# A gated recurrence feeding a squared-ReLU MLP: y with tokens as rows and then transposed, against y formed in channels

## The chip, the cores and the metric

The kernel runs on one core of a Trainium2 chip. TensorE multiplies matrices: it loads up to 128x128 stationary weights (PEld in the profile) and streams a moving operand past them into PSUM. VectorE (DVE), ScalarE (ACT) and GpSimd (POOL) work on tiles, and DMA queues, most of them issued by SyncE (SP), move data. The metric is device microseconds from start to end of one execution. Before the change the median of three runs is 202.72 us (202.46 to 202.79).

## The reference

Four batches, eight heads, 768 steps, head size 48; the outputs of the recurrence are the 3072 tokens of an MLP with 384 channels and 2048 hidden units.

```python
def _attn_ref(q, k, v, alpha):
    state = np.zeros((B, H, D, D))
    for t in range(S):
        state = alpha[:, :, t, :, None] * state + np.einsum('bhd,bhe->bhde', k[:, :, t], v[:, :, t])
        y[:, :, t] = np.einsum('bhd,bhde->bhe', q[:, :, t], state)

def _moe_ref(x, w_in, w_out, s, b):
    h = x @ w_in
    r = np.maximum(h, 0.0)
    g = s * (r * r) + b
    return g @ w_out
```

## The kernel before, in words

**Blocks.** The 768 steps of a batch are cut into six chunks of 128 tokens, so there are 24 blocks, `n = 0..23`, with chunk number `c = n % 6`. A block's recurrence is done with matrix products. The weights w_in and w_out are loaded once, cast to bf16 and kept.

**One block.** `ln` (ScalarE) takes the logarithm of alpha; `cum` sums it over the tokens with a triangular matmul and ScalarE forms exp(-sum) and exp(sum), L233 and L234; `qk` (VectorE, L250 and L251) scales k and q with them; `tr` transposes q and k to have channels as partitions (eight TensorE transposes, L256, one VectorE copy, L261); `amat` forms the products A of q and k, 128x128 for each head, with two heads side by side in the rows of the array (L271), and VectorE masks them into `am_sb` (L279). `vcast` (GpSimd, L211 and L215) casts v to bf16 into two zero-padded tiles.

**y and the state.** `inter` (L287, not for c = 0) and `yp` (L306) make y directly with channels as partitions in the bank `y_ps`. For `inter` the state of the chunk before, spread with zeros over six 128x128 slices of `sd_sb`, is the weight and the transposed q is moving: six matmuls of 128 columns. For `yp` the padded v is the weight (64 columns, so two matmuls run beside each other in two halves of the array's columns) and A is moving: twelve matmuls of 128 columns. For c < 5, eight small matmuls (L331) form each head's product of k and v in `p_ps`; `state` adds it to the decayed state (VectorE, L350 or L352) and GpSimd scales it (L358, L364, L371). ScalarE copies y to `xd_sb` (L339). Because of the padding, the order of y's channels differs from that of x, and the rows of w_in are loaded in the same order: `load_w_in` cuts w_in into two halves of columns and each half into four DMAs by rows.

**The MLP.** For a unit u = 0..3 of a block, `mp` computes four hidden tiles of 128 into a bank of `h_ps` (two in turn; twelve matmuls, L393), `rl` is the ReLU on ScalarE (L407), `sq` the square on VectorE (L414), and `mm2` (called as `o`) adds four of the sixteen products with w_out into `o_ps` (L428). After the last unit VectorE adds the bias row (L441), or, for the first five blocks, ScalarE keeps the sum (L437) until the bias is known.

**Order.** Each engine runs its instructions in the order in which they are written. That order is fixed by hand: a list for the first four blocks, with positions 0.1 apart, and formulas after that, with eight positions for a block (p = 8n). From block 8 on, between y(n) at p and y(n+1) at p + 8 lie amat(n+1) at p + 0.1, o(n-1,0) at p + 0.5, cum(n+2) at p + 1.2, m(n,0) at p + 1.5, then o and m in turn, and tr(n+2) at p + 5.2. `busy(i)` puts i matmuls without a use (L197) where TensorE would stand still early on. Loads for eight blocks are in flight on SP's queue; w_in follows blocks 0 and 1, with its second half between the four loads of block 2.

Of the kernel before, what the change touches and what calls it, by code (L numbers as in the profile page):

```python
# [14 lines left out]
def kernel(  # L20
# [165 lines left out]
    def bias_row():  # L186
        for part, c0, c1 in ((p_ps[:, 192:512], 0, 320), (y_ps[:, 384:448], 320, 384)):
            nc.tensor.matmul(out=part, lhsT=ones_f, rhs=cs_sb[:, 0, c0:c1], start=True, stop=True)
            nc.scalar.activation(out=bias_w[:, c0:c1], in_=part, func=AF.Copy, scale=b_col)
# [19 lines left out]
    def vcast(n):  # L209
        vs = v_sb[n % NLD]  # L210
        nc.gpsimd.tensor_copy(  # L211
            out=vp_sb[n % 3].rearrange("s h (a b) -> s h a b", b=4)[:, :, :, 0:3],
            in_=vs[:, 0:6].rearrange("s h (a b) -> s h a b", b=3),
        )
        nc.gpsimd.tensor_copy(  # L215
            out=vz_sb[n % 3].rearrange("s e t (a b) -> s e t a b", b=4)[:, :, :, :, 3],
            in_=vs[:, 6:8].rearrange("s e (a t) -> s e t a", t=3),
        )
# [62 lines left out]
    def inter(n):  # L281
        if n % NCH == 0:
            return
        sd = sd_sb[(n - 1) % 2]
        for i in range(6):
            p, kk = (i, i) if i < 3 else (3, i - 3)
            nc.tensor.matmul(  # L287
                out=y_ps[:, 128 * kk : 128 * kk + 128],
                lhsT=sd[0:112, i, :],
                rhs=qkT_sb[n % 2][0:112, 0, p, :],  # L290
                start=(i == 0),
                stop=False,
                skip_group_check=True,
            )

# [3 lines left out]

    def yp(n):  # L300
        c = n % NCH
        first = [c == 0, c == 0]

        def y(h, kk, lhsT, last):
            e = h % 2
            nc.tensor.matmul(  # L306
                out=y_ps[64 * e : 64 * e + 64, 128 * kk : 128 * kk + 128],
                lhsT=lhsT,
                rhs=am_sb[e][n % 2][:, h // 2, :],
                start=first[e],  # L310
                stop=last,
                skip_group_check=True,
            )
            first[e] = False

        for kk in range(3):
            for e in range(2):
                y(2 * kk + e, kk, vp_sb[n % 3][:, 2 * kk + e, :], False)
        for kk in range(3):
            for e in range(2):  # L320
                y(6 + e, kk, vz_sb[n % 3][:, e, kk, :], True)
        if c < NCH - 1:
            kb = kb_sb[n % 3]
            for p in range(NP):
                for e in range(2):
                    h = 2 * p + e
                    if h < 6:
                        rhs = vp_sb[n % 3][:, h].rearrange("s (a b) -> s a b", b=4)[:, :, 0:3]
                    else:
                        rhs = vz_sb[n % 3][:, e].rearrange("s t (a b) -> s t a b", b=4)[:, :, :, 3]  # L330
                    nc.tensor.matmul(  # L331
                        out=pst[64 * e : 64 * e + 48, p, :],
                        lhsT=kb[:, h, 0:48],
                        rhs=rhs,
                        start=True,
                        stop=True,
                    )
# [1 line left out]
        nc.scalar.activation(  # L339
            out=xd_sb[g][:, :, i * C : (i + 1) * C],  # L340
            in_=y_ps[:, 0:384].rearrange("a (t s) -> a t s", t=KT),
            func=AF.Copy,
        )
        if c < NCH - 1:
            state(n)

    def state(n):
        c = n % NCH
        if c == 0:
            nc.vector.tensor_copy(out=t1_sb[0:112], in_=pst[0:112])  # L350
        else:
            nc.vector.tensor_tensor(out=t1_sb[0:112], in0=pst[0:112], in1=sc_sb[0:112], op=ALU.add)  # L352
        bl = blast[n % 3]
        sd = sd_sb[n % 2]
        for e in range(2):
# [2 lines left out]
            nc.gpsimd.tensor_tensor(  # L358
                out=cols[:, 0:3, :, 0:3],
                in0=t1_sb[r, 0:3].rearrange("k p (a b) -> k p a b", b=3),  # L360
                in1=bl[r, 0:3].unsqueeze(3).to_broadcast([48, 3, 16, 3]),
                op=ALU.mult,
            )
            nc.gpsimd.tensor_tensor(  # L364
                out=cols[:, 3:6, :, 3],
                in0=t1_sb[r, 3].rearrange("k (t a) -> k t a", t=3),
                in1=bl[r, 3:4].to_broadcast([48, 3, 16]),
                op=ALU.mult,
            )
# [218 lines left out]
```

## Time and profile before

| what | value |
|---|---|
| median of three runs | 202.72 us |
| the profiled execution: its time | 202.63 us |
| its span, first to last instruction | 200.9 us |
| granted TensorE clock, mean | 0.996 |
| VectorE busy | 149.4 us, 74% |
| ScalarE busy | 106.5 us, 53% |
| GpSimd busy | 77.6 us, 39% |
| HBM read, written | 25.19 MB, 4.74 MB |

A matmul's time in the profile runs until its result is out, and the next one starts long before that. So the time that a matmul occupies the array is read from the distance between starts, not from its own length. Idle time of an engine costs nothing unless somebody waits for what it does next.

### The profile page before, as it was taken

What the parts mean: (1) busy time and instruction counts of PE and PEld (TensorE: products, weight loads), DVE (VectorE), ACT (ScalarE), POOL (GpSimd) and SP (SyncE); (2) the same over time, 40 slices, a digit from 0 to 9 for tenths busy, and PEclk for the clock granted to TensorE, in tenths of its full rate; (3) what the DMA queues carried; (4) which work ended last, traced back from release to release, by engine and by line L of the source; (5) the groups of instructions that cost most, each with busy time, mean ns of one, the idle gap of its engine ahead of it and who ended that gap; (6) DMA issues with size and microseconds to landing.
All of it is one profiled execution on the core that took longest, in us unless ns stands there. A gap on an engine that the chain in (4) does not pass through costs nothing.

```text
span 200.9 us, 6383 instructions
## 1 busy us (share of the span) xinstructions
PE 187.6 (93%) x2574; PEld 146.4 (73%) x2577; DVE 149.4 (74%) x289; ACT 106.5 (53%) x211; POOL 77.6 (39%) x171
## 2 busy tenths in 40 slices
PE   1979899999988999999999999999999999999992
PEld 1546588765775788888788878888878887888771
DVE  6456687788699779999886877887777787796341
ACT  3225486663557464655555565465565556544440
POOL 8364332530620078437530633641701463362000
PEclk9999999999999999999999999999999999999998
DMA  7999999999999546939695965983998591111102
GB/s 127 194 301 300 241 231 380 226 196 191 173 190 170 80 73 90 204 78 195 120 233 125 227 115 109 185 132 70 219 173 136 85 186 40 43 39 42 41 5 76
DMA packets 112608, 30.35 MB, mean 151 GB/s; under 512 B 106675, under 2 KB 111810, under 8 KB 112578
## 3 DMA queue, kind: packets, MB, share of 16 engines
q1 hardware_dynamic: 112574, 29.94, 74.6%
q8 instruction: 20, 0.33, 0.8%
q14 instruction: 10, 0.08, 0.1%
q10 hardware_dynamic: 4, 0.00, 0.0%
HBM read 25.19 MB, written 4.74 MB: 149 GB/s over the span
## 4 chain that ended last, share of the span: by engine, by line
PE 79%; DVE 8%; ACT 3%; issue 3%; DMA 2%; SPq 1%; POOL 1%; DVEq 0%; ACTq 0%; POOLq 0%
PE h_ps L393 28%; PE o_ps L428 26%; PE ct_ps L256 6%; PE y_ps L306 5%; PE a_ps L271 4%; PE y_ps L287 3%; PE a_ps L428 2%; ACT r_sb L407 2%; DMA al_sb<-in_alpha_dram 2%; DVE qkT L261 2%; PE o_ps L197 2%; PE ct_ps L222 1%; DVE qb_sb L251 1%; PE p_ps L331 1%; DVE kb_sb L250 1%
## 5 line engine op out<-in xcount | busy, mean ns | idle before, releaser
L407 ACT ACTIVATE r_sb<-h_ps 128x512 bf16<-128x512 f32 x94 | 56.1, 599 | 48.2 <-PE h_ps L393 47.7
L393 PE MATMUL h_ps<-xd_all,w_in_bf 128*128 128x128 bf16 x1128 | 77.3, 219 | 0.2 <-ACT xd_all L339 0.2
L393 PEld LDWEIGHTS <-w_in_bf 128*128 128x128 bf16 x1152 | 70.5, 98 | 9.0 <-ACT w_in_bf L158 0.5
L414 DVE TENSOR_TENSOR gt_all<-r_sb 128x512 bf16<-128x512 bf16 x96 | 49.2, 516 | 32.1 <-ACT r_sb L407 31.3
L428 PE MATMUL o_ps<-w_out_bf,gt_all 128*128 128x384 bf16 x336 | 68.4, 327 | 0.0
L358 POOL TENSOR_TENSOR sd_sb<-t_sb,blast 48x144 bf16<-48x144 f32 x40 | 19.0, 475 | 93.3 <-DVE t_sb L352 53.9
L428 PEld LDWEIGHTS <-gt_all 128*128 128x128 bf16 x384 | 33.2, 98 | 16.1
L233 ACT ACTIVATE bi_sb<-ct_ps 128x384 f32<-128x384 f32 x24 | 11.8, 490 | 17.1 <-PE ct_ps L222 13.4
L261 DVE COPY qkT<-ct_ps 112x1024 bf16<-112x1024 bf16 x24 | 16.5, 687 | 5.1 <-PE ct_ps L256 3.4
L211 POOL CAST vp_sb<-v_sb 128x288 bf16<-128x288 f32 x24 | 15.2, 633 | 11.8 <-DMA v_sb<-in_v_dram 11.6
L339 ACT ACTIVATE xd_all<-y_ps 128x384 bf16<-128x384 f32 x24 | 11.8, 490 | 11.5 <-PE y_ps L306 9.5
L279 DVE TENSOR_TENSOR am_a<-a_ps,mask 128x512 bf16<-128x512 f32 x24 | 16.4, 683 | 1.5 <-PE a_ps L271 1.5
L250 DVE TENSOR_TENSOR kb_sb<-k_sb,bi_sb 128x384 bf16<-128x384 f32 x24 | 13.9, 577 | 3.7 <-ACT bi_sb L233 2.7
L251 DVE TENSOR_TENSOR qb_sb<-q_sb,b_sb 128x384 bf16<-128x384 f32 x24 | 16.4, 682 | 0.0
L279 DVE TENSOR_TENSOR am_b<-a_ps,mask 128x512 bf16<-128x512 f32 x24 | 16.3, 680 | 0.0
L364 POOL TENSOR_TENSOR sd_sb<-t_sb,blast 48x48 bf16<-48x48 f32 x40 | 15.6, 389 | 0.0
L207 ACT ACTIVATE la_sb<-al_sb 128x384 bf16<-128x384 f32 x24 | 12.4, 516 | 3.6 <-DMA al_sb<-in_alpha_dram 3.6
L256 PEld LDWEIGHTS <-qb_sb 128*112 128x112 bf16 x96 | 8.7, 133 | 6.7 <-DVE qb_sb L251 4.6
L222 PE MATMUL ct_ps<-la_sb,U_bf 128*128 128x384 bf16 x24 | 8.0, 332 | 4.8 <-ACT la_sb L207 4.8
L215 POOL CAST vz_sb<-v_sb 128x96 bf16<-128x96 f32 x24 | 12.2, 509 | 0.0
L256 PE MATMUL ct_ps<-ident,qb_sb 128*112 128x128 bf16 x96 | 9.8, 226 | 2.2 <-DVE qb_sb L251 2.0
L234 ACT ACTIVATE b_sb<-ct_ps 128x384 f32<-128x384 f32 x24 | 11.7, 486 | 0.0
(69 smaller groups left out, 206.7 us busy)
## 6 DMA issues: line engine op xcount, KB each, us to landing
al_sb<-in_alpha_dram SPq DMA_DIRECT2D x24, 192.0 KB, 3.2
k_sb<-in_k_dram SPq DMA_DIRECT2D x24, 192.0 KB, 3.7
q_sb<-in_q_dram SPq DMA_DIRECT2D x24, 192.0 KB, 4.7
v_sb<-in_v_dram SPq DMA_DIRECT2D x24, 192.0 KB, 4.5
out_dram<-out_sb SPq DMA_DIRECT2D x19, 192.0 KB, 1.9
w_in_st<-in_moe_w_in_dram SPq DMA_DIRECT2D x8, 384.0 KB, 8.7
w_out_st<-in_moe_w_out_dram SPq DMA_DIRECT2D x4, 768.0 KB
out_dram<-keep_sb SPq DMA_DIRECT2D x5, 192.0 KB
```

The lines of the kernel that those rows point to most:

```text
L211: nc.gpsimd.tensor_copy(out=vp_sb[n % 3].rearrange("s h (a b) -> s h a b", b=4)[:, :, :, 0:3], in_=vs[:, 0:6].rearrange("s h (a b) -> s h ...
L250: nc.vector.tensor_tensor(out=kb_sb[n % 3][:, :, 0:48], in0=k_sb[n % NLD], in1=bi_sb[n % 2], op=ALU.mult)
L251: nc.vector.tensor_tensor(out=qb_sb[n % 2][:, :, 0:48], in0=q_sb[n % NLD], in1=b_sb[n % 2], op=ALU.mult)
L256: nc.tensor.transpose(out=t_ps[0:112, x, p, :], in_=t.rearrange("a h d -> a (h d)")[:, 128 * p : 128 * p + 112], identity=ident,)
L261: nc.vector.tensor_copy(out=qkT_sb[n % 2][0:112].rearrange("a x p t -> a (x p t)"), in_=t_ps[0:112].rearrange("a x p t -> a (x p t)"),)
L279: nc.vector.tensor_tensor(out=am_sb[e][n % 2], in0=a_ps[e], in1=mask4, op=ALU.mult)
L358: nc.gpsimd.tensor_tensor(out=cols[:, 0:3, :, 0:3], in0=t1_sb[r, 0:3].rearrange("k p (a b) -> k p a b", b=3), in1=bl[r, 0:3].unsqueeze(3). ...
L364: nc.gpsimd.tensor_tensor(out=cols[:, 3:6, :, 3], in0=t1_sb[r, 3].rearrange("k (t a) -> k t a", t=3), in1=bl[r, 3:4].to_broadcast([48, 3, ...
L393: nc.tensor.matmul(out=hp[:, jj * N : (jj + 1) * N], lhsT=w_in_bf[:, kk, 128 * j : 128 * (j + 1)], rhs=xd_sb[g][:, kk, 0:N], start=(kk == ...
L407: nc.scalar.activation(out=rs, in_=h_of.pop((g, u)), func=AF.Relu)
L414: nc.vector.tensor_tensor(out=gt_sb[g][:, u * 512 : (u + 1) * 512], in0=rs, in1=rs, op=ALU.mult)
L428: nc.tensor.matmul(out=op[:, 0:d_model], lhsT=gt_sb[g][:, j * N + t * C : j * N + (t + 1) * C], rhs=w_out_bf[:, j, :], start=(j == 0), sto ...
```

## The change

y is formed with tokens as partitions. In `yp` the transposed q and the masked A become the weights, and the state (96 columns for two heads) and v (48 columns for one head) are moving. A new ScalarE copy puts y into `y_bf`; a new step `xt` transposes it in three TensorE transposes into one of the two `h_ps` banks, and ScalarE copies that to `xd_sb`. The products of k and v are made for two heads at once (four matmuls of 128x96, of which the diagonal blocks are used), so `t1_sb`, `sc_sb` and `p_ps` are 96 columns wide for each pair, and `sd_sb` has four slices of 96. v is cast by one GpSimd instruction without padding, and six memsets of the padded tiles and one of `p_ps` go. w_in is loaded in its own row order by quarters of columns: two whole quarters, then two quarters in halves of 64 rows between the loads of block 2. The bias row is made in three pieces of 128 columns. The order by hand is rewritten: `xt(n)` stands at p + 1.0, o(n-1,1) moves from p + 2.5 to p + 1.5, m(n,0) from p + 1.5 to p + 2.5, and in the opening list 39 matmuls without a use become 31, the first cast of w_in stands ahead of y(1), and `qk(1)` ahead of the state of block 0.

```diff
-    def load_w_in(half, r):
-        cols = slice(half * d_ff // 2, (half + 1) * d_ff // 2)
-        if r < 3:
-            rows = moe_w_in[0 : 96 * KT, cols].rearrange("(t a b) f -> b a t f", t=KT, b=3)[r]
-        else:
-            rows = moe_w_in[96 * KT :, cols].rearrange("(i t) f -> i t f", t=KT)
-        nc.sync.dma_start(out=w_in_st[r::4, :, cols], in_=rows)
+    def load_w_in(i, r0=0, r1=128):
+        cols = slice(i * d_ff // 4, (i + 1) * d_ff // 4)
+        nc.sync.dma_start(
+            out=w_in_st[r0:r1, :, cols],
+            in_=moe_w_in[:, cols].rearrange("(t r) f -> r t f", t=KT)[r0:r1],
+        )
...
     def vcast(n):
...
+        nc.gpsimd.tensor_copy(out=v_bf[n % 3], in_=v_sb[n % NLD])
...
     def yp(n):
         c = n % NCH
+        if c > 0:
+            for p in range(NP):
+                nc.tensor.matmul(
+                    out=y_ps[:, 96 * p : 96 * p + 96],
+                    lhsT=qkT_sb[n % 2][0:112, 0, p, :],
+                    rhs=sd_sb[(n - 1) % 2][0:112, p, :],
...
+        for h in range(H):
             nc.tensor.matmul(
+                out=y_ps[:, 48 * h : 48 * h + 48],
+                lhsT=am_sb[h % 2][n % 2][:, h // 2, :],
+                rhs=v_bf[n % 3][:, h, :],
...
         if c < NCH - 1:
+            kb = kb_sb[n % 3].rearrange("a h d -> a (h d)")
             for p in range(NP):
+                nc.tensor.matmul(
+                    out=pst[:, p, :],
+                    lhsT=kb[:, 128 * p : 128 * p + 128],
+                    rhs=v_bf[n % 3][:, 2 * p : 2 * p + 2, :],
...
+        nc.scalar.activation(out=y_bf[n % 2], in_=y_ps[:, 0 : H * 48], func=AF.Copy)
+
+    def xt(n):
+        hp = h_ps[nrelu[0] % 2].bitcast(BF16)[:, 0 : KT * C]
+        nrelu[0] += 1
+        for kk in range(KT):
+            nc.tensor.transpose(
+                out=hp[:, kk * C : (kk + 1) * C],
+                in_=y_bf[n % 2][:, 128 * kk : 128 * (kk + 1)],
+                identity=ident,
+            )
         g, i = group_of[n]
         nc.scalar.activation(
             out=xd_sb[g][:, :, i * C : (i + 1) * C],
-            in_=y_ps[:, 0:384].rearrange("a (t s) -> a t s", t=KT),
+            in_=hp.rearrange("a (t s) -> a t s", t=KT),
...
         for e in range(2):
+            r, d = slice(64 * e, 64 * e + 48), slice(48 * e, 48 * e + 48)
             nc.gpsimd.tensor_tensor(
+                out=sd[r, :, d], in0=t1_sb[r, :, d], in1=bl[r].to_broadcast([48, NP, 48]), op=ALU.mult
             )
...
-    for r in range(4):
-        load_w_in(0, r)
+    load_w_in(0)
+    load_w_in(1)
     for r, ld in enumerate((load_a, load_k, load_q, load_v)):
         ld(2)
-        load_w_in(1, r)
+        load_w_in(2 + r // 2, 64 * (r % 2), 64 * (r % 2) + 64)
...
-            (ln, 0), (vcast, 0), (cum, 0), (qk, 0), (spread,), (busy, 4), (tr, 0), (busy, 2), (ln, 1), (vcast, 1), (amat, 0),
-            (busy, 3), (cum, 1), (y, 0), (qk, 1), (busy, 3), (tr, 1), (busy, 3), (amat, 1), (busy, 5), (y, 1),
-            (win, 0), (win, 1), (ln, 2), (busy, 4), (m, 0, 0), (m, 1, 0), (cum, 2), (m, 0, 1), (mr, 1, 1), (vcast, 2),
+            (ln, 0), (vcast, 0), (cum, 0), (qk, 0), (spread,), (busy, 3), (tr, 0), (busy, 1), (ln, 1), (vcast, 1), (amat, 0),
+            (cum, 1), (busy, 3), (yp, 0), (qk, 1), (st, 0), (busy, 1), (tr, 1), (xt, 0), (busy, 2), (amat, 1), (win, 0),
+            (busy, 5), (yp, 1), (mr, 0, 0), (st, 1), (win, 1), (xt, 1), (ln, 2), (sq, 0, 0), (busy, 1), (m, 0, 1), (m, 1, 0),
+            (cum, 2), (mr, 1, 1), (vcast, 2),
...
         for u in range(4):
-            at(p + 1.5 + 2 * u, m, n, u)
-            at(p + 8.5 + 2 * u, o, n, u)
+            at(p + (2.5, 3.5, 5.5, 7.5)[u], m, n, u)
+            at(p + (8.5, 9.5, 12.5, 14.5)[u], o, n, u)
+        at(p + 1.0, xt, n)
```

More of the change, by code (lines that the diff above doesn't have):

```diff
@@ L62 @@
     p_ps = ps.tile([128, 512], FP32, name="p_ps")
-    pst = p_ps[:, 0:NP * 48].rearrange("a (p e) -> a p e", p=NP)
+    pst = p_ps[:, 0:NP * 96].rearrange("a (p e) -> a p e", p=NP)
     h_ps = [ps.tile([128, 512], FP32, name=f"h_ps{i}") for i in range(2)]
@@ L88 @@
     kb_sb = ring("kb_sb", [128, H, 64], BF16, 3)
-    vp_sb = ring("vp_sb", [128, 6, 64], BF16, 3)
-    vz_sb = ring("vz_sb", [128, 2, 3, 64], BF16, 3)
+    v_bf = ring("v_bf", [128, H, 48], BF16, 3)
+    y_bf = ring("y_bf", [128, H * 48], BF16, 2)
     qkT_sb = ring("qkT", [128, 2, NP, 128], BF16, 2)
@@ L94 @@
     row_dr = [dr.tile([1, H * 48], FP32, name=f"row_dr{i}") for i in range(3)]
-    t1_sb = sb.tile([128, NP, 48], FP32, name="t1_sb")
-    sc_sb = sb.tile([128, NP, 48], FP32, name="sc_sb")
-    sd_sb = ring("sd_sb", [128, 6, 128], BF16, 2)
+    t1_sb = sb.tile([128, NP, 96], FP32, name="t1_sb")
+    sc_sb = sb.tile([128, NP, 96], FP32, name="sc_sb")
+    sd_sb = ring("sd_sb", [128, NP, 96], BF16, 2)
     r_sb = ring("r_sb", [128, 512], BF16, 6)
@@ L184, in bias_sum, with bias_row @@
         nc.vector.tensor_tensor(out=cs_sb[:, 0], in0=cs_sb[:, 0], in1=cs_sb[:, 1], op=ALU.add)
[L186 to L189, printed above, removed]
+    def bias_row(i):
+        part, c = (y_ps, p_ps, y_ps)[i][:, 384:512], slice(128 * i, 128 * i + 128)
+        nc.tensor.matmul(out=part, lhsT=ones_f, rhs=cs_sb[:, 0, c], start=True, stop=True)
+        nc.scalar.activation(out=bias_w[:, c], in_=part, func=AF.Copy, scale=b_col)
     def spread():
@@ L209, in vcast @@
     def vcast(n):
[L210 to L218, printed above, removed]
+        nc.gpsimd.tensor_copy(out=v_bf[n % 3], in_=v_sb[n % NLD])
     def cum(n):
@@ L279, in amat @@
             nc.vector.tensor_tensor(out=am_sb[e][n % 2], in0=a_ps[e], in1=mask4, op=ALU.mult)
[L281 to L294, printed above, removed]
     group_of = []
@@ L301, in yp @@
         c = n % NCH
[L302 to L311, printed above, removed]
+        if c > 0:
[4 more added lines that the diff above has]
+                    rhs=sd_sb[(n - 1) % 2][0:112, p, :],
+                    start=(p == 0),
+                    stop=False,
+                    skip_group_check=True,
+                )
@@ L312, in y @@
+        for h in range(H):
+            nc.tensor.matmul(
+                out=y_ps[:, 48 * h : 48 * h + 48],
+                lhsT=am_sb[h % 2][n % 2][:, h // 2, :],
+                rhs=v_bf[n % 3][:, h, :],
+                start=(c == 0 and h == 0),
+                stop=(h == H - 1),
                 skip_group_check=True,
             )
[L314 to L318, printed above, removed]
@@ L319, in yp @@
-        for kk in range(3):
-            for e in range(2):
-                y(6 + e, kk, vz_sb[n % 3][:, e, kk, :], True)
         if c < NCH - 1:
-            kb = kb_sb[n % 3]
+            kb = kb_sb[n % 3].rearrange("a h d -> a (h d)")
             for p in range(NP):
[L325 to L337, printed above, removed]
+                nc.tensor.matmul(
+                    out=pst[:, p, :],
+                    lhsT=kb[:, 128 * p : 128 * p + 128],
+                    rhs=v_bf[n % 3][:, 2 * p : 2 * p + 2, :],
+                    start=True,
+                    stop=True,
+                )
@@ L338, in yp @@
+        nc.scalar.activation(out=y_bf[n % 2], in_=y_ps[:, 0 : H * 48], func=AF.Copy)
[7 more added lines that the diff above has]
+                identity=ident,
+            )
         g, i = group_of[n]
@@ L340, in yp, with st @@
             out=xd_sb[g][:, :, i * C : (i + 1) * C],
-            in_=y_ps[:, 0:384].rearrange("a (t s) -> a t s", t=KT),
+            in_=hp.rearrange("a (t s) -> a t s", t=KT),
             func=AF.Copy,
         )
-        if c < NCH - 1:
+    def st(n):
+        if n % NCH < NCH - 1:
             state(n)
@@ L355, in state @@
         for e in range(2):
-            r = slice(64 * e, 64 * e + 48)
-            cols = sd[r, :, 64 * e : 64 * e + 64].rearrange("k i (a b) -> k i a b", b=4)
+            r, d = slice(64 * e, 64 * e + 48), slice(48 * e, 48 * e + 48)
             nc.gpsimd.tensor_tensor(
[L359 to L368, printed above, removed]
+                out=sd[r, :, d], in0=t1_sb[r, :, d], in1=bl[r].to_broadcast([48, NP, 48]), op=ALU.mult
             )
@@ L371, in state @@
             nc.gpsimd.tensor_tensor(
-                out=sc_sb[0:112], in0=t1_sb[0:112], in1=bl[0:112].to_broadcast([112, NP, 48]), op=ALU.mult
+                out=sc_sb[0:112], in0=t1_sb[0:112], in1=bl[0:112].to_broadcast([112, NP, 96]), op=ALU.mult
             )
@@ L475 @@
         make_upper_triangular(nc, mask4[:, i], 1.0, diag=True)
-    for t in vp_sb + vz_sb:
-        nc.gpsimd.memset(t, 0.0)
-    nc.vector.memset(p_ps, 0.0)
     for t in sd_sb:
@@ L489, in y @@
     def y(n):
-        inter(n)
         yp(n)
+        st(n)
     def wout(i):
@@ L513 @@
         [
-            (ln, 0), (vcast, 0), (cum, 0), (qk, 0), (spread,), (busy, 4), (tr, 0), (busy, 2), (ln, 1), (vcast, 1), (amat, 0),
-            (busy, 3), (cum, 1), (y, 0), (qk, 1), (busy, 3), (tr, 1), (busy, 3), (amat, 1), (busy, 5), (y, 1),
-            (win, 0), (win, 1), (ln, 2), (busy, 4), (m, 0, 0), (m, 1, 0), (cum, 2), (m, 0, 1), (mr, 1, 1), (vcast, 2),
+            (ln, 0), (vcast, 0), (cum, 0), (qk, 0), (spread,), (busy, 3), (tr, 0), (busy, 1), (ln, 1), (vcast, 1), (amat, 0),
+            (cum, 1), (busy, 3), (yp, 0), (qk, 1), (st, 0), (busy, 1), (tr, 1), (xt, 0), (busy, 2), (amat, 1), (win, 0),
+            (busy, 5), (yp, 1), (mr, 0, 0), (st, 1), (win, 1), (xt, 1), (ln, 2), (sq, 0, 0), (busy, 1), (m, 0, 1), (m, 1, 0),
+            (cum, 2), (mr, 1, 1), (vcast, 2),
             (qk, 2), (sq, 1, 1), (busy, 6), (tr, 2), (busy, 3), (amat, 2), (win, 2), (win, 3), (busy, 5), (y, 2), (ln, 3),
-            (mr, 0, 2), (mr, 1, 2), (cum, 3), (vcast, 3), (sq, 0, 2), (sq, 1, 2), (qk, 3), (mr, 2, 0), (mr, 0, 3), (mr, 1, 3),
+            (mr, 0, 2), (xt, 2), (mr, 1, 2), (cum, 3), (vcast, 3), (sq, 0, 2), (sq, 1, 2), (qk, 3), (mr, 2, 0), (mr, 0, 3), (mr, 1, 3),
             (tr, 3), (sq, 2, 0), (mr, 2, 1), (sq, 0, 3), (amat, 3), (sq, 1, 3), (sq, 2, 1), (mp, 2, 2), (wout, 0), (mp, 2, 3),
-            (busy, 1), (y, 3), (rl, 2, 2), (rl, 2, 3), (sq, 2, 2), (sq, 2, 3), (wout, 1), (o, 0, 0), (o, 1, 0), (o, 2, 0),
+            (busy, 1), (yp, 3), (rl, 2, 2), (rl, 2, 3), (st, 3), (sq, 2, 2), (sq, 2, 3), (wout, 1), (o, 0, 0), (xt, 3), (o, 1, 0), (o, 2, 0),
             (m, 3, 0), (m, 3, 1), (wout, 2), (o, 0, 1), (o, 1, 1), (colsum, 1), (m, 3, 2),
@@ L531 @@
     at(47.4, bias_sum)
-    at(51.2, bias_row)
+    for i in range(3):
+        at(51.2 + i, bias_row, i)
     for n in range(NKEEP):
-        at(52.5 + 8 * n, add_bias, n)
-        at(55.0 + 8 * n, store, n, keep_sb[n])
+        at(53.7 + 8 * n, add_bias, n)
+        at(56.2 + 8 * n, store, n, keep_sb[n])
     for u in range(4):
-        at((30.5, 31.5, 34.5, 36.5)[u], o, 3, u)
+        at((30.5, 31.5, 33.5, 36.5)[u], o, 3, u)
     at(20.0, load, NLD)
```

## The prediction

> **What bounds it now.** First the page's shares of engines and the busy times by stretch, then TensorE's timeline over one block, then ScalarE's.
>
> ```profile
> PE 187.6 (93%) x2574; PEld 146.4 (73%) x2577; DVE 149.4 (74%) x289; ACT 106.5 (53%) x211; POOL 77.6 (39%) x171
> ```
>
> ```profile
> core 0: us, PE busy (x) PEld busy (x) DVE busy (x) ACT busy (x) POOL busy (x), PEclk, DMA share, GB/s
> 0.00:27.00 27.00, 20.24 (x221) 12.95 (x225) 16.80 (x44) 10.79 (x24) 13.16 (x38) 1.00 1.05 228
> ...
> 116.95:124.20 7.25, 7.25 (x111) 5.92 (x109) 6.09 (x13) 4.28 (x9) 3.27 (x7) 1.00 0.75 138
> 124.20:189.00 64.80, 64.80 (x957) 52.69 (x956) 49.49 (x96) 35.27 (x69) 24.61 (x54) 1.00 0.58 106
> ```
>
> From block 4 on (y(4) starts at 49.72) TensorE is hardly ever free: 7.25 of 7.25 us in the block of 116.95, at a granted clock of 1.00, with VectorE busy for 6.09 of it. There the kernel is as long as its matmul stream, so each term is the distance between starts. Up to 27 us it is otherwise: DMA engines are full, and 38 of 39 matmuls without a use lie there.
>
> ```profile
> 116.28 0.83 PE L393 MATMUL h_ps<-xd_all,w_in_bf 128*128 128x128 bf16 x12
> 116.95 0.50 PE L287 MATMUL y_ps<-qkT,sd_sb 112*128 112x128 bf16 x6
> 117.38 0.24 PE L306 MATMUL y_ps<-am_a,vp_sb 128*64 128x128 bf16 x1
> ...
> 117.74 0.25 PE L331 MATMUL p_ps<-vp_sb,kb_sb 128*48 128x48 bf16 x6
> 117.83 0.21 PE L331 MATMUL p_ps<-vz_sb,kb_sb 128*48 128x48 bf16 x2
> 117.97 0.40 PE L271 MATMUL a_ps<-qkT 48*128 48x128 bf16 x8
> 118.30 0.82 PE L428 MATMUL o_ps<-w_out_bf,gt_all 128*128 128x384 bf16 x4
> 118.96 0.33 PE L222 MATMUL ct_ps<-la_sb,U_bf 128*128 128x384 bf16 x1
> 119.12 0.83 PE L393 MATMUL h_ps<-xd_all,w_in_bf 128*128 128x128 bf16 x12
> ...
> 121.76 0.39 PE L256 MATMUL ct_ps<-ident,qb_sb 128*112 128x128 bf16 x4
> 121.98 0.39 PE L256 MATMUL ct_ps<-ident,kb_sb 128*112 128x128 bf16 x4
> ```
>
> The first column is the start, the second runs until the results are out. Steps: L393, 12 in 0.67 us (116.28 to 116.95), 56 ns each with 128 moving columns; L428, 4 in 0.66, 165 ns each with 384; so a column costs (165 - 56) / 256 = 0.43 ns. Four transposes step 0.22, 56 ns each. L331 goes in pairs, three pairs in 0.09, 30 ns a pair. L287 takes 0.43, of which 6 x 0.056 = 0.34 is its own: the other 0.09 goes before the first matmul of 64-column weights. Likewise 0.14 from the last L331 pair to L271, 0.11 over the pair's own 0.03; and L271's 0.33 has 0.10 over its four pairs of 0.056. So a change of the array's partition costs some 0.1 us, three times a block.
>
> ```profile
> 117.21 0.60 ACT L407 ACTIVATE r_sb<-h_ps 128x512 bf16<-128x512 f32 x1
> 117.95 0.49 ACT L339 ACTIVATE xd_all<-y_ps 128x384 bf16<-128x384 f32 x1
> 119.32 0.49 ACT L233 ACTIVATE bi_sb<-ct_ps 128x384 f32<-128x384 f32 x1 [0.88 <-PE ct_ps L222]
> ```
>
> ScalarE copies y at 117.95; its user, m(n,0), starts at 119.12. This distance now has to hold a second copy and a transpose.
>
> **TensorE, block by block.** Before, from the last m to amat: 1.02 us with both state and `inter` (116.95 to 117.97), 0.68 for c = 0 (110.04 to 110.72), 0.89 for c = 5 (102.92 to 103.81). After:
> - `inter` and the products of k and v, four matmuls of 96 columns each: 56 - 32 x 0.43 = 42 ns, 0.17 us each group.
> - `yp`, eight of 48 columns, each with a fresh 128-column load. No row shows that. From below: 56 - 80 x 0.43 = 22 ns. From above: 56 ns, as the same load with 128 moving columns. I take 30 ns, the step of L331, the nearest row with 48 moving columns: 0.24 us.
> - one partition change instead of two up to amat: 0.11. That of amat's end stays.
> - `xt`: three transposes at 56 ns, 0.17. They have the form of L256.
>
> That is 0.17 + 0.24 + 0.17 + 0.11 + 0.17 = 0.86 for a middle block (saves 0.16), 0.69 for c = 0 (saves nothing) and 0.69 for c = 5 (saves 0.20). Blocks 4 to 23 hold 13 middle ones, 3 with c = 0 and 4 with c = 5: 13 x 0.16 + 4 x 0.20 = 2.9 us. Blocks 2 and 3 are middle ones in a stretch that is mostly TensorE too: 0.3.
>
> [...]
>
> **The longer way from y to xd.** Counted from the end of m(n-1,3), M = 116.95: its ReLU starts at M + 0.26 and holds ScalarE for about 0.5, so the y copy starts near M + 0.75 and is done at 1.24, seen by TensorE at 1.3 (as 50.72 + 0.49 was followed by L393 at 51.26). TensorE reaches xt at 0.69 + 0.33 (amat) + 0.65 (o) = M + 1.67, for c = 0 and 5 about M + 1.5: covered by amat and o(n-1,0). After xt starts, m(n,0) may start when the third transpose is out (0.11 + 0.22), ScalarE woken (0.05), copied (0.49) and TensorE woken (0.05): 0.92. TensorE has xt 0.17, cum 0.16 and the moved o 0.65 to do, 0.98. A slack of 0.06 us, so I take nothing, and keep 0 to 0.3 a block (rival 2). The cover is missing at the end: block 22 has no cum (0.1), block 23 no amat, state or cum: xt waits 0.25 and m 0.1. Together +0.45. cum(n+2)'s two exponentials stand behind the new copy, up to 0.2 later against M; qb then ends about 0.5 us before tr(n+2), which stays at p + 5.2: covered.
>
> **Other engines.** VectorE's t1 is 384 columns wide, not 192: by L441 (128x384 f32 from PSUM, 549 ns) against 352, +0.2 a block, 6.3 of 7.1 us; covered by what is left, 0.2 a block if not. ScalarE gets 24 x 0.49 = 11.8 us, some 60% of the span. GpSimd: two scalings of 192 columns by about 0.5 (L371, 192 wide, 638; L358, 144 wide, 475) for four that took 1.7; sc near 1.0 (L448, 384 wide, 995 ns) for 0.64; one cast by 0.85 (633 x 384/288) for 1.14: no more than before, and due only a block later. SP issues six w_in transfers for eight, with the same bytes; packets of 2 KB for 4 KB. The bias row (1.0 us of TensorE) and the kept stores move by about one position: nothing waits for them. No cost for these.
>
> **The opening.** tr(0) starts at 7.29 behind four fillers of 0.42, though qb ends at 6.75: three fillers give 6.9, 0.4 sooner. VectorE's order then was am_b to 11.0, a wait for the state products, t1, and k, q of block 1 until 13.0, tr(1) at 13.06. With qk(1) ahead of t1: 10.6 + 1.0, so tr(1) near 11.7, 1.3 sooner, and amat(1), y(1) with it. The first m started at 18.05 behind casts that started at 17.37 after y; with one quarter cast ahead of y(1), near 16. But block 2 meets transfers: GpSimd waited until 24.04 for its v, ScalarE until 25.24 for the second half of w_in. So y(2), whose A ended at 26.22, gets to about 25 at best (1.2 to 1.4 sooner), and ln(3), behind the last cast, from 27.30 to about 26.3. I take 1.0 us, between 1.5 and -0.5 (a loss, as the copies of y are two more ScalarE pieces ahead of those casts).
>
> **Sum.** -2.9 - 0.3 + 0.45 - 1.0 = -3.8: span 197.1, time 202.63 - 3.8 = 198.8. The run profiled is 0.09 under the median, so the median answers to about 198.9; I keep 198.8.
>
> **Rivals.**
> 1. *Weight loads set the step of short matmuls* (slower). If the load and not the moving columns fills the 56 ns, all sixteen short matmuls step 56: 0.22 + 0.45 + 0.22 + 0.11 + 0.17 = 1.17 for a middle block (+0.15), 0.95 for c = 0 (+0.27) and c = 5 (+0.06): 13 x 0.15 + 3 x 0.27 + 4 x 0.06 = +3.0 in place of -2.9, and +0.3 for -0.3: 205.3. It decides from a step of about 53 ns in `yp` alone (3.8 us over 8 x 20 matmuls is 24 ns). For it: each 128-column load here steps 56. Against: so do L306's pairs, with 128 columns moving, which points to the columns.
> 2. *ScalarE's second copy is late for m(n,0)*. The slack is 0.06. If copy and handovers take 0.3 more (the wide VectorE copy out of PSUM, L261, needs 0.69 for its bf16 against 0.49), each of 20 blocks stands 0.24 us: +4.8, 203.6. For it: two handovers in a row; against: the 0.49 is the same in all 24 copies.
> 3. *VectorE becomes the bound*, or the opening loses its gain: 6.3 of 7.1 us in strict order; with the 0.2 of t1 exposed in 16 blocks (3.2) the time is 202.0, or 202.6 with waits that follow. Against: o(n,u) is due a block after its square.
> 4. *Transposes that do not overlap*. If each of xt's three holds TensorE for its own length, 0.22 us (four of L256 take 0.39, less three steps of 0.056), a block loses 3 x 0.165 = 0.5, and 22 blocks 10.9: 209.7. Against: L256's rows, a step of 56 ns at a clock of 1.00. [...]
>
> **Chances.** Forecast 0.70, rival 1 0.10, rival 2 0.10, rival 3 0.09, rival 4 0.01. About 0.2% (0.4 us) can be told from no change. Rivals 1, 2 and 4 are slower (0.21); of rival 3 0.04 is faster and 0.05 the same, and 0.01 of the forecast's far end goes to the same: faster 0.73, same 0.06, slower 0.21. The forecast's own range is 196.6 (steps of 22 ns, 1.3 less; an opening of 1.5, 0.5 less; nothing lost at the end, 0.4 less) to 201.4 (steps of 40 ns, 1.6 more; no gain early, 1.0 more). The range reaches on to rival 2's price and stops short of rival 1's: 196.4 to 203.7.
>
> **What would show it.** Period of a middle block 7.09 for 7.25; the sixteen matmuls ahead of amat in 0.58 us and a single gap of 0.11; xt's three 0.17 apart from cum, and no idle time of TensorE ahead of m(n,0); first m near 16 us, y(4) about 1.3 sooner. Wrong if the 48-column matmuls step over 45 ns, if TensorE idles by over 0.1 before xt or m(n,0), or if y(4) is not sooner than 49.7.

## The result, and the profile after

The changed kernel takes 210.7 us (median of six runs, 209.55 to 211.88), against 202.72 (202.46 to 202.86) for the kernel before beside it: a ratio of 1.0394, with a 95% interval of 1.036 to 1.0428. It is slower by 3.9%; 198.8 was predicted, and even the upper end of the range, 203.7, was passed. The profiled execution took 210.76 us with a span of 209.0, against 202.63 and 200.9. Of the runs below only f1 had slow executions, two of its ten (552.5 us at a granted clock of 0.352, and 205.81); its median and ratio are of the other eight.

The page's shares of engines, after, with its row of granted clocks:

```profile
PE 188.4 (90%) x2427; PEld 145.2 (69%) x2427; DVE 156.4 (75%) x288; ACT 116.7 (56%) x236; POOL 62.4 (30%) x101
...
PEclk9999859999999999999999999999999999999999
```

Busy times by stretch, after, in the columns of the table of before; the second row is one block from y to y:

```profile
core 0: us, PE busy (x) PEld busy (x) DVE busy (x) ACT busy (x) POOL busy (x), PEclk, DMA share, GB/s
0.00:27.00 27.00, 18.62 (x163) 12.22 (x164) 14.38 (x38) 11.22 (x24) 8.07 (x24) 0.96 1.12 206
126.88:133.98 7.10, 7.10 (x104) 5.71 (x102) 6.14 (x12) 4.43 (x9) 2.91 (x4) 1.00 0.73 141
133.98:189.00 55.02, 55.02 (x780) 44.67 (x778) 46.77 (x86) 34.47 (x70) 20.67 (x28) 1.00 0.52 103
```

The late block does what was forecast: TensorE has no gap, and a block takes 7.10 us where it took 7.25. The first 27 us do not: 163 matmul records for 221, and a granted clock of 0.96 for 1.00. That mean leaves out the time ahead of the trace's first record of the clock, and there TensorE is slow too: a matmul without a use (a filler, L191 after, L197 before) takes 0.63 us up to 14.8 us here and 0.38 after that, where before the change the fillers are down to 0.38 from 8.4 on. TensorE's timeline in the block of 126.88:

```profile
126.88 0.34 PE L276 MATMUL y_ps<-sd_sb,qkT 112*128 112x96 bf16 x4
127.05 0.19 PE L285 MATMUL y_ps<-v_bf,am_a 128*128 128x48 bf16 x1
127.08 0.18 PE L285 MATMUL y_ps<-v_bf,am_b 128*128 128x48 bf16 x1
...
127.26 0.33 PE L296 MATMUL p_ps<-v_bf,kb_sb 128*128 128x96 bf16 x4
127.52 0.40 PE L257 MATMUL a_ps<-qkT 48*128 48x128 bf16 x8
127.85 0.82 PE L398 MATMUL o_ps<-w_out_bf,gt_all 128*128 128x384 bf16 x4
128.51 0.33 PE L310 MATMUL h_ps<-ident,y_bf 128*128 128x128 bf16 x3
128.68 0.33 PE L208 MATMUL ct_ps<-la_sb,U_bf 128*128 128x384 bf16 x1
```

Up to amat (L257) it takes 0.64 where it took 1.02, and the new transposes (L310) take 0.17, with no idle time in brackets at any of them. ScalarE's part of the way from y to the MLP, same block, with idle time and releaser in brackets:

```profile
127.63 0.48 ACT L303 ACTIVATE y_bf<-y_ps 128x384 bf16<-128x384 f32 x1
128.88 0.49 ACT L316 ACTIVATE xd_all<-h_ps 128x384 bf16<-128x384 bf16 x1 [0.76 <-PE h_ps L310]
```

So the loss was made earlier. The starts of y(n), the first matmul into `y_ps`, place it (read from the timelines, us):

| | y(2) | y(4) | y(7) | y(11) | y(23) | span |
|---|---|---|---|---|---|---|
| before | 25.91 | 49.72 | 73.86 | 102.92 | 188.34 | 200.9 |
| after | 30.38 | 54.92 | 80.63 | 113.15 | 196.69 | 209.0 |
| after - before, in the stretch | +4.47 | +0.73 | +1.57 | +3.46 | -1.88 | -0.2 |

(The last column is from y(23) to the end; spans are given to a tenth.) Three places lose: the opening (5.20 up to y(4)), blocks 4 to 6 (1.57) and blocks 7 to 10 (3.46). The twelve blocks from 11 on gain 1.88; the forecast's terms for them give 1.68.

**The opening.** Who waited ahead of block 2, after, in the timelines of VectorE, GpSimd, ScalarE and TensorE:

```profile
24.81 0.56 DVE L237 TENSOR_TENSOR qb_sb<-q_sb,b_sb 128x384 bf16<-128x384 f32 x1 [2.65 <-DMA q_sb<-in_q_dram]
```

```profile
27.96 0.50 POOL L204 CAST v_bf<-v_sb 128x384 bf16<-128x384 f32 x1 [7.76 <-DMA v_sb<-in_v_dram]
```

```profile
29.68 0.63 ACT L152 ACTIVATE w_in_bf<-w_in_st 128x512 bf16<-128x512 f32 x1 [5.70 <-DMA w_in_st<-in_moe_w_in_dram]
```

```profile
25.42 0.67 PE L242 MATMUL ct_ps<-ident,qb_sb 128*112 128x128 bf16 x4 [2.56 <-DVE qb_sb L237]
25.89 0.63 PE L242 MATMUL ct_ps<-ident,kb_sb 128*112 128x128 bf16 x4
...
28.27 2.31 PE L191 MATMUL o_ps<-mask,U_bf 128*128 128x512 bf16 x5
```

Before, TensorE's timeline at the same place:

```profile
23.06 0.43 PE L256 MATMUL ct_ps<-ident,qb_sb 128*112 128x128 bf16 x4 [0.42 <-DVE qb_sb L251]
...
24.83 1.25 PE L197 MATMUL o_ps<-mask,U_bf 128*128 128x512 bf16 x5
```

Block 2's q, v and the last quarter of w_in all land late. TensorE starts tr(2) at 25.42, before at 23.06: 2.36 later. Having stood idle for 2.56, it then runs slowly: four transposes step 0.47 us (25.42 to 25.89) where they took 0.26, and five fillers take 2.31 where they took 1.25. That costs another 2.1 between tr(2) and y(2) (4.96 for 2.85). The granted clock of 27 to 52 us is 0.90: in the trace's clock record it is 0.5 from 25.03 to 31.86.

The SP queue carries the same bytes in fewer, but differently placed pieces. The time of one packet, read from the trace by piece (medians for the pieces; means for the 192 B packets, which are the q, k, v and alpha loads in flight beside the piece):

```
before   4096 B, every fourth partition      median 159-166 ns    192 B beside it: mean 15 ns
after    2048 B, all 128 partitions          median 84-86 ns
after    2048 B, 64 neighbouring partitions  median 160-174 ns    192 B beside it: mean 24-29 ns
```

A half of neighbouring partitions, 0 to 63 or 64 to 127, takes twice the time per packet (160-174 ns for 84-86), and the small loads beside it are slower (24-29 ns for 15). They are not slow through such pieces alone: before the first packet of w_in starts, four small loads in a row (4.8 to 8.9 us, before and after) also take 22 to 24 ns a packet on average.

**Blocks 7 to 10.** Three periods, from y(7) to y(10), of 8.49 us in place of 7.25. VectorE, GpSimd and TensorE there, after, in their timelines:

```profile
92.50 2.58 DVE L237 TENSOR_TENSOR qb_sb<-q_sb,b_sb 128x384 bf16<-128x384 f32 x1
```

```profile
92.14 1.13 POOL L341 TENSOR_TENSOR sc_sb<-t_sb,blast 112x384 f32<-112x384 f32 x1
93.22 0.50 POOL L204 CAST v_bf<-v_sb 128x384 bf16<-128x384 f32 x1
93.68 0.99 POOL L418 TENSOR_TENSOR keep_sb<-keep_sb,bias_w 128x384 f32<-128x384 f32 x1
```

```profile
95.14 0.43 PE L242 MATMUL ct_ps<-ident,qb_sb 128*112 128x128 bf16 x4 [1.25 <-DVE qb_sb L237]
```

VectorE's scaling of q holds it for 2.58 us, and ends (95.08) 0.41 after the end (94.67) of GpSimd's third instruction in a row, the bias addition to a kept block; the transposes wait 1.25 for it. Before, the same place, VectorE and then GpSimd:

```profile
84.59 0.86 DVE L251 TENSOR_TENSOR qb_sb<-q_sb,b_sb 128x384 bf16<-128x384 f32 x1
85.37 2.18 DVE L414 TENSOR_TENSOR gt_all<-r_sb 128x512 bf16<-128x512 bf16 x2
```

```profile
84.36 0.67 POOL L371 TENSOR_TENSOR sc_sb<-t_sb,blast 112x192 f32<-112x192 f32 x1
84.98 0.75 POOL L211 CAST vp_sb<-v_sb 128x288 bf16<-128x288 f32 x1
85.68 0.40 POOL L215 CAST vz_sb<-v_sb 128x96 bf16<-128x96 f32 x1
85.94 0.99 POOL L448 TENSOR_TENSOR keep_sb<-keep_sb,bias_w 128x384 f32<-128x384 f32 x1
```

There `sc` was half as wide and done 0.44 after the scaling of q began, which got through in 0.86. The stall was there too, on the first of two squares (1.85 us, and 2.18 for both), and TensorE lost nothing by it: that block too took 7.25.

**Blocks 4 to 6** are in the experiments e3 and f2.

### The profile page after: what moved, and what is told of

It is laid out like the page before. It is cut to its first block, busy times and chain, and to the rows that moved or that the text cites. A ratio compares the mean times of both kernels' runs of the same rounds, so it can differ in the third digit from the quotient of the medians.

```text
span 209.0 us, 6036 instructions
## 1 busy us (share of the span) xinstructions
PE 188.4 (90%) x2427; PEld 145.2 (69%) x2427; DVE 156.4 (75%) x288; ACT 116.7 (56%) x236; POOL 62.4 (30%) x101
## 4 chain that ended last, share of the span: by engine, by line
PE 69%; SPq 9%; DVE 8%; DMA 7%; ACT 4%; issue 3%; DVEq 0%; ACTq 0%
PE h_ps L363 25%; PE o_ps L398 22%; PE ct_ps L242 5%; DMA q_sb<-in_q_dram 4%; PE a_ps L398 3%; DVE qb_sb L237 3%; SPq L140 3%; PE a_ps L257 3%; ACT r_sb L377 3%; PE y_ps L285 2%; PE h_ps L310 2%; PE o_ps L191 2%; PE y_ps L276 1%; DMA row_dr<-b_sb 1%; PE ct_ps L208 1%
## 5 line engine op out<-in xcount | busy, mean ns | idle before, releaser
L363 PE MATMUL h_ps<-xd_all,w_in_bf 128*128 128x128 bf16 x1128 | 75.0, 219 | 1.4 <-ACT w_in_bf L152 0.8
L363 PEld LDWEIGHTS <-w_in_bf 128*128 128x128 bf16 x1152 | 69.4, 98 | 8.0 <-ACT w_in_bf L152 1.2
L384 DVE TENSOR_TENSOR gt_all<-r_sb 128x512 bf16<-128x512 bf16 x96 | 45.6, 488 | 30.3 <-ACT r_sb L377 29.8
L337 POOL TENSOR_TENSOR sd_sb<-t_sb,blast 48x192 bf16<-48x192 f32 x40 | 20.6, 515 | 107.4 <-DVE t_sb L332 57.6
L237 DVE TENSOR_TENSOR qb_sb<-q_sb,b_sb 128x384 bf16<-128x384 f32 x24 | 24.3, 1013 | 2.6 <-DMA q_sb<-in_q_dram 2.6
L204 POOL CAST v_bf<-v_sb 128x384 bf16<-128x384 f32 x24 | 16.3, 683 | 19.7 <-DMA v_sb<-in_v_dram 18.5
L316 ACT ACTIVATE xd_all<-h_ps 128x384 bf16<-128x384 bf16 x24 | 11.7, 489 | 14.4 <-PE h_ps L310 14.4
L341 POOL TENSOR_TENSOR sc_sb<-t_sb,blast 112x384 f32<-112x384 f32 x16 | 18.2, 1137 | 1.3
L303 ACT ACTIVATE y_bf<-y_ps 128x384 bf16<-128x384 f32 x24 | 11.7, 486 | 6.7 <-PE y_ps L285 6.7
L191 PE MATMUL o_ps<-mask,U_bf 128*128 128x512 bf16 x31 | 12.5, 523 | 0.0
```

The costliest lines, as they stand in the source:

```text
L191: nc.tensor.matmul(out=o_ps, lhsT=U_bf, rhs=mask4.rearrange("a p t -> a (p t)"), start=True, stop=True,)
L204: nc.gpsimd.tensor_copy(out=v_bf[n % 3], in_=v_sb[n % NLD])
L237: nc.vector.tensor_tensor(out=qb_sb[n % 2][:, :, 0:48], in0=q_sb[n % NLD], in1=b_sb[n % 2], op=ALU.mult)
L337: nc.gpsimd.tensor_tensor(out=sd[r, :, d], in0=t1_sb[r, :, d], in1=bl[r].to_broadcast([48, NP, 48]), op=ALU.mult)
L341: nc.gpsimd.tensor_tensor(out=sc_sb[0:112], in0=t1_sb[0:112], in1=bl[0:112].to_broadcast([112, NP, 96]), op=ALU.mult)
L363: nc.tensor.matmul(out=hp[:, jj * N : (jj + 1) * N], lhsT=w_in_bf[:, kk, 128 * j : 128 * (j + 1)], rhs=xd_sb[g][:, kk, 0:N], start=(kk == ...
```

## The experiments

Each was timed beside the kernel before; ratios are to it. The y(n) starts of all follow below f4.

**e1: the halves on every second partition** in place of 64 neighbours; bytes, order and packet size stay. (`load_w_in` takes a slice of rows for it.)

```diff
-        load_w_in(2 + r // 2, 64 * (r % 2), 64 * (r % 2) + 64)
+        load_w_in(2 + r // 2, slice(r % 2, 128, 2))
```

> The changed kernel, but each half of the last two quarters of w_in takes every second row (64 partitions spread over all 128) instead of 64 neighbouring rows; same number of transfers, packets of 2 KB and bytes. Theory A (64 neighbouring partitions are reached at half the rate, so the opening waits for q, v and w_in of block 2): q of block 2 lands near 22 us instead of 24.8, the last quarter near 25 instead of 29.7, y(4) starts near 49.5 instead of 54.9, time near 205.3. Rival (the 2 KB packets or the number of descriptors are what is slow): nothing moves, 210.7, and a 2 KB packet still takes some 175 ns between 16 and 28 us. The stall of blocks 8 to 10 stays in both.

Measured: 206.24 us, 1.015 (1.0135 to 1.0165). The packets of all four halves have a median of 84 to 88 ns, the 192 B packets beside them a mean of 15 ns. The granted clock is 1.00 in 0 to 27 and 27 to 52 us, and y(4) starts at 49.92, 5.00 sooner than after. VectorE's and ScalarE's timelines at block 2:

```profile
21.56 0.56 DVE L237 TENSOR_TENSOR qb_sb<-q_sb,b_sb 128x384 bf16<-128x384 f32 x1 [0.37 <-ACT r_sb L377]
```

```profile
24.62 0.63 ACT L152 ACTIVATE w_in_bf<-w_in_st 128x512 bf16<-128x512 f32 x1 [2.57 <-DMA w_in_st<-in_moe_w_in_dram]
```

q no longer ends the wait, and the last quarter is there 5.06 us sooner. It follows that the placement of the rows alone made the loss of the opening: 4.9 of the 8.1 us of span. Blocks 7 to 10 still take 32.52, and the time is above the 205.3 expected.

**b1: the same placement put into the kernel before**, whose quarters of rows then go to 32 neighbouring partitions each (the rows of w_in no longer match y's channels).

```diff
-        nc.sync.dma_start(out=w_in_st[r::4, :, cols], in_=rows)
+        nc.sync.dma_start(out=w_in_st[32 * r : 32 * r + 32, :, cols], in_=rows)
```

> The kernel before, but each of the eight pieces of w_in is put on 32 neighbouring partitions instead of every fourth one; the rows of w_in then do not match the order of y's channels, with the same work and bytes otherwise. Theory A: the same slow transfers, with 4 KB packets at over 300 ns instead of 204, y(4) 4 to 6 us later than 49.7 and a time of 207 to 209. Rival (2 KB packets): 202.7.

Measured: 210.62 us, 1.0364 (1.0339 to 1.0388). Packets of 4096 B go from 159-166 ns to 306-331, the small ones beside them from a mean of 15 to 24-28. TensorE at tr(2):

```profile
28.99 0.43 PE L256 MATMUL ct_ps<-ident,qb_sb 128*112 128x128 bf16 x4 [4.39 <-DVE qb_sb L251]
```

It stands idle for 4.39 us, its clock is then 0.93 in 27 to 52 us, and y(2) starts at 33.22. One edit of placement, and no other part of the change, takes 7.4 us, more than the 207 to 209 expected.

**f1: pieces of 64 that straddle the middle.** Made on e3 (below): one piece is partitions 32 to 95, the others 0 to 31 and 96 to 127. This asks whether it is the count of neighbours that matters, or the half of the memory in which they lie.

```diff
-        load_w_in(2 + r // 2, slice(r % 2, 128, 2))
+        for rows in ((slice(32, 96),), (slice(0, 32), slice(96, 128)))[r % 2]:
+            load_w_in(2 + r // 2, rows)
```

> The kernel with both mended (strided rows, additions on VectorE: 201.9), but each of the last two quarters of w_in goes first to partitions 32 to 95 in one piece of 64 neighbouring rows, then to 0 to 31 and to 96 to 127 in two pieces. Theory A1 (partitions below 64 and from 64 on have separate ways in, and a piece that lies in one of them gets half): the first piece runs at 100 to 110 ns a packet of 2 KB like strided rows, the two others at about 175, so half of the loss: y(4) near 52.5 instead of 50.2, time near 204.3. [...] Theory A2 (any neighbouring rows are slow): all pieces at 175 ns or more, y(4) near 55, 207. Theory A3 (only fewer than 128 rows in a piece matters) is already out with the strided run.

Measured: 203.5 us, 1.0022 (1.0005 to 1.004). Partitions 32 to 95, 64 neighbours, move at 89 ns a packet (91 in the next quarter) with a mean of 15 (17) for the small ones beside them; 0 to 31 take 167 and 166, 96 to 127 take 138 and 148. So the pieces that lay in one half, 0 to 63 or 64 to 127, were slow here (138 to 167 ns), and not because their partitions were neighbours (64 of them moved at 89). Separate ways in for the two halves, as theory A1 has them, are not shown by this. The total was 0.8 us better than expected; why the two end pieces cost less here than the halves did is open. The small packets beside 0 to 31 took only 15.7 and 16.5 ns on average, beside 96 to 127 they took 22.5 and 25.7.

**e2: the five bias additions left out** of the changed kernel (its first five blocks are stored without the bias row).

```diff
-        at(53.7 + 8 * n, add_bias, n)
```

> The changed kernel without the five additions of the bias row on GpSimd; the first five blocks are stored without the bias row. Theory B (VectorE's scaling of q, L237, cannot finish while GpSimd runs scaling, cast and this addition one behind the other): L237 takes at most 1.2 us in blocks 8 to 10 instead of 2.58, their period falls from 8.49 to about 7.1, time 210.7 - 3 x 1.35 = 206.7. Rival (the wider state products alone stretch it): L237 stays over 2 us and the time at 210.7.

Measured: 207.78 us, 1.0209 (1.0178 to 1.024). The periods from y(7) to y(11) come to 28.33, where after has 32.52 and before 29.06: the loss is gone and the block's gain is there. VectorE, then GpSimd, at that place:

```profile
93.67 1.18 DVE L237 TENSOR_TENSOR qb_sb<-q_sb,b_sb 128x384 bf16<-128x384 f32 x1
```

```profile
93.32 1.12 POOL L341 TENSOR_TENSOR sc_sb<-t_sb,blast 112x384 f32<-112x384 f32 x1
94.39 0.83 POOL L204 CAST v_bf<-v_sb 128x384 bf16<-128x384 f32 x1
```

With two GpSimd instructions in a row, not three, the scaling of q takes 1.18 for 2.58, and ends (94.85) 0.41 after the end (94.44) of the first. In time the kernel gained 2.9 us on after; set against the kernel before beside each, 1.0209 for 1.0394, it is some 3.8, of the 4.19 that the periods show. The profiled run, the slowest of four, had a longer opening still, though its order there is that of after: its halves of w_in took 190 to 196 ns a packet, and y(4) is at 57.36 for 54.92.

```profile
27.42 0.68 PE L242 MATMUL ct_ps<-ident,qb_sb 128*112 128x128 bf16 x4 [5.45 <-DVE qb_sb L237]
```

**e3: e1, and the additions on VectorE**, a position where nothing queues behind them.

```diff
-        nc.gpsimd.tensor_tensor(out=keep_sb[n], in0=keep_sb[n], in1=bias_w, op=ALU.add)
+        nc.vector.tensor_tensor(out=keep_sb[n], in0=keep_sb[n], in1=bias_w, op=ALU.add)
...
-        at(53.7 + 8 * n, add_bias, n)
-        at(56.2 + 8 * n, store, n, keep_sb[n])
+        at(62.9 + 8 * n, add_bias, n)
+        at(65.4 + 8 * n, store, n, keep_sb[n])
```

> Both mended, and the whole result computed: rows of w_in taken as in the strided run, and the five additions on VectorE, behind the last unit's product of a block, instead of on GpSimd. If A and B are separate and add up: 210.7 - 5.4 - 4.0 = 201.3, a little faster than before (202.7). If the loss of blocks 5 to 10 only moves to other blocks: 204 to 205. An addition of 0.55 on VectorE in five blocks is in the first figure at nothing.

Measured: 201.9 us, 0.9933 (0.9915 to 0.995): faster than the kernel before. Both causes are gone together, and 0.7 of span is what remains to the good: +0.45 up to y(4), +1.69 to y(7), -0.73 to y(11), -1.86 to y(23), -0.2 at the end. TensorE's timeline, one line of block 2 and then block 4:

```profile
27.66 0.83 PE L363 MATMUL h_ps<-xd_all,w_in_bf 128*128 128x128 bf16 x12 [0.52 <-ACT r_sb L377]
...
50.17 0.34 PE L276 MATMUL y_ps<-sd_sb,qkT 112*128 112x96 bf16 x4
...
51.49 0.34 PE L310 MATMUL h_ps<-ident,y_bf 128*128 128x128 bf16 x3 [0.41 <-ACT y_bf L303]
51.67 0.33 PE L208 MATMUL ct_ps<-la_sb,U_bf 128*128 128x384 bf16 x1
...
54.22 0.43 PE L242 MATMUL ct_ps<-ident,qb_sb 128*112 128x128 bf16 x4 [0.90 <-DVE qb_sb L237]
```

In blocks 4 to 6, `cum` of the next block comes at once behind `xt` and its tr follows 2.5 us later, not a block later. `cum` waits for `xt`, which waits 0.41 for ScalarE's copy of y; its exponentials then stand on ScalarE behind the second copy (`bi` of block 5 starts 2.09 after y(4), before 1.39), and tr(5) waits 0.90.

**f2: cum(5) ahead of xt(4)**, on e3.

```diff
-        at(p + 1.0, xt, n)
+        at(p + (1.05 if n == 4 else 1.0), xt, n)
```

> The kernel with both mended, but xt(4) stands behind cum(5) instead of ahead of it. Theory C (where the next block's scaling is made in the same block, the copy, transpose and second copy of y delay ScalarE's exponentials and with them the scaled q, which TensorE waits for): the scaled q of block 5 ends about 1 us sooner, TensorE's wait of 0.90 ahead of tr(5) goes, y(5) 0.8 sooner, time 200.9 to 201.3 for 201.9. Rival (VectorE's work as a whole is what is late in blocks 5 to 7): y(7) no sooner, 201.9.

Measured: 201.5 us, 0.9911 (0.9888 to 0.9933). TensorE:

```profile
51.35 0.33 PE L208 MATMUL ct_ps<-la_sb,U_bf 128*128 128x384 bf16 x1
...
51.92 0.34 PE L310 MATMUL h_ps<-ident,y_bf 128*128 128x128 bf16 x3 [0.25 <-ACT y_bf L303]
...
53.73 0.39 PE L242 MATMUL ct_ps<-ident,qb_sb 128*112 128x128 bf16 x4
...
66.50 0.43 PE L242 MATMUL ct_ps<-ident,qb_sb 128*112 128x128 bf16 x4 [1.24 <-DVE qb_sb L237]
```

tr(5) waits for nothing, and y(4) to y(5) is 6.88 in place of 7.84 (before 6.93). That names the cause in block 4, and gives back 0.91 of e3's 1.69 between y(4) and y(7). In blocks 5 and 6 the other 0.78 is left, with a wait of 1.24 before tr(7) (before 0.71), as in e3; its cause was not tried. The time, expected at 200.9 to 201.3, is not told apart from e3's.

**f3: xt(2) moved behind m(1,2)**, on e3. In the opening `xt` takes one of the two `h_ps` banks, and m(1,2) waits 0.52 for a ReLU to free one.

```diff
-            (mr, 0, 2), (xt, 2), (mr, 1, 2), (cum, 3), (vcast, 3), (sq, 0, 2), (sq, 1, 2), (qk, 3), (mr, 2, 0), (mr, 0, 3), (mr, 1, 3),
+            (mr, 0, 2), (mr, 1, 2), (cum, 3), (vcast, 3), (sq, 0, 2), (sq, 1, 2), (qk, 3), (xt, 2), (mr, 2, 0), (mr, 0, 3), (mr, 1, 3),
```

> The kernel with both mended, but xt(2) stands behind qk(3), right ahead of the unit m(2,0) that needs it, instead of between two units of the MLP. Theory D (xt takes one of the two banks of h_ps, so the unit behind it waits for a ReLU that stands on ScalarE behind the copy of y and a logarithm): the wait of 0.52 ahead of m(1,2) goes, y(3) starts 0.5 to 0.9 sooner than 34.5, and the time is 201.2 to 201.5. Rival (the opening is paced by transfers later on, so what is won there is lost by y(4)): y(4) stays at 50.2, 201.9.

Measured: 201.94 us, 0.9945 (0.9929 to 0.9962), no gain on e3. The wait of 0.52 is gone, and a longer one has come, for the same copy:

```profile
27.71 0.33 PE L310 MATMUL h_ps<-ident,y_bf 128*128 128x128 bf16 x3
...
29.41 0.83 PE L363 MATMUL o_ps<-xd_all,w_in_bf 128*128 128x128 bf16 x12 [1.38 <-ACT xd_all L316]
```

y(2) to y(3) is 9.69 with it, 9.29 without, 8.41 before. The theory that moving `xt` frees this time falls: the longer way from y to xd was waited for at both places tried.

**f4: f2 and f3 together.**

> Both moves of xt together. If C and D are separate: 200.4 to 200.8, some 1.3% under the kernel before. If one takes the other's gain: 201.0 to 201.4.

Measured: 201.54 us, 0.9926 (0.9909 to 0.9943). That meets neither sum (200.4 to 200.8, or 201.0 to 201.4). The intervals of e3, f2, f3 and f4 overlap, so these four are not told apart; f2 has the lowest ratio.

| | y(2) | y(4) | y(7) | y(11) | y(23) | span |
|---|---|---|---|---|---|---|
| e1 | 25.03 | 49.92 | 75.72 | 108.24 | 191.78 | 204.1 |
| b1 | 33.22 | 57.33 | 81.86 | 111.19 | 196.60 | 209.1 |
| f1 | 25.36 | 50.80 | 76.63 | 104.96 | 188.51 | 201.0 |
| e2 | 32.38 | 57.36 | 83.20 | 111.53 | 195.09 | 207.4 |
| e3 | 25.22 | 50.17 | 76.00 | 104.33 | 187.89 | 200.2 |
| f2 | 25.91 | 50.60 | 75.52 | 103.85 | 187.40 | 199.7 |
| f3 | 25.09 | 50.13 | 75.84 | 104.17 | 187.72 | 200.0 |
| f4 | 24.74 | 50.02 | 74.94 | 103.27 | 186.81 | 199.1 |

Each row is one execution, and the opening differs between them even where the order is the same: y(2) by 0.9 among e1, e3 and f2, by 2.0 between after and e2. One thing that differs is when TensorE's clock comes up: the trace's first record of a full clock is at 14.79 us in after and 14.12 in e3, and between 8.29 and 9.68 in the other eight. It is not what made y(2) late: in e2 it is at 9.50, and y(2) at 32.38.

## Why the prediction was wrong

**TensorE's terms were right.** The 48-column matmuls step 25.5 ns (30 taken, 22 to 56 allowed), the 96-column ones 43 (42), `xt` takes 0.17 (0.17), and the sixteen with the one partition change 0.64 (0.69). Six blocks in a row take 42.06 us for 43.02: 0.96 saved, 0.84 by the terms. Rival 1 (weight loads set the step) and rival 4 (transposes do not overlap) fall with these steps.

**The slack of 0.06 held** where it was counted: no idle time ahead of m(n,0) from block 11 on, so rival 2 falls there. The end was counted too dear: `xt` of the last block waited 0.13 and m 0.09, and the stretch from y(23) on got 0.2 shorter.

**The failed step with the largest price** is "SP issues six w_in transfers for eight, with the same bytes; packets of 2 KB for 4 KB", put at nothing by "No cost for these." It counted transfers, bytes and packet sizes, not which partitions they go to. 64 partitions of one half moved at half the rate (160 to 174 ns a packet for 84 to 86), and it was the opening, of which the prediction itself said that the DMA engines are full and GpSimd and ScalarE wait for transfers, that paid: 2.36 us of waiting and 2.1 at a low clock up to y(2). Rival 3 had "the opening loses its gain" at no more than 202.6; a loss was allowed only through ScalarE's copies.

**The second** is "GpSimd: ... no more than before, and due only a block later", with "qb then ends about 0.5 us before tr(n+2), which stays at p + 5.2: covered". GpSimd's sum was right (2.91 us of a block, before 3.27). But its instructions were costed by length alone, and a wider `sc` ends later against the scaling of q. Three instructions then stood back to back where the bias addition came behind scaling and cast, and the cover was lost in three periods, at 1.24 us each.

**The third** is the same cover, worked out for a middle block and then used for "Blocks 4 to 23". In blocks 4 to 6 the next block's exponentials and transposes are due in the same block, so no such cover was there: 1.57 us were lost, where the terms had promised a gain of some 0.4. That the second copy was on the path is shown for block 4 alone (f2); for the rest of it, in blocks 5 and 6, the cause is open.

**The opening's gain** was mis-sized even without the first loss. The first m came early enough: at 16.80 in after and 16.46 in e3, where the clock came up late, and at 15.22 to 15.84 in the other traces of the new order ("near 16" forecast, 18.05 before). But with the rows strided y(2) starts 0.88 (e1), 0.69 (e3) and 0.00 (f2) sooner than before, where 1.2 to 1.4 was forecast, and each of the three then loses 0.88 or 0.89 in block 2. Two waits of TensorE in e3, 0.52 ahead of m(1,2) (before none) and 0.26 ahead of tr(3) (before 0.11), make up 0.67 of that. Blocks 2 and 3, "0.3" to the good, cost 0.88 to 1.14. The prediction's own test, y(4) sooner than 49.7, came out against it in every run.

**One reading of rival 1.** In the trace of before a load's own row (PEld L393) takes 98 ns on average, while load and matmul together step 56. So the loads overlap with matmuls, and the step says nothing of how long a load takes.

With both large causes out, the change is worth 0.7% (e3) to 0.9% (f2), not 1.9%.

## What to carry to other kernels

When a load is cut into pieces, look at which partitions each piece reaches, not only at its bytes and packets; here pieces on every second partition took 84 to 88 ns a packet of 2048 B, as pieces on all 128 did (84 to 86), and those on every fourth 159 to 166 one of 4096 B; halves of neighbours took 160 to 174 for 2048 B, and the 192 B packets beside these a mean of 24 to 29 for 15. When an instruction on GpSimd gets wider, look at what VectorE is about to start beside it, and at how many GpSimd instructions stand queued back to back; an instruction that costs nothing where nobody waits for its victim can cost time when another comes to stand there, as the bias addition did here: nothing before the change, 1.24 us in each of three periods after it. A slack worked out for the steady block has to be worked out again for each stretch whose order differs.
